# Values laid out block-diagonally, so that one matmul serves two heads

## The chip, the cores and the metric

The kernel runs on one core of a Trainium2 chip. The metric is the device time of one execution in microseconds. Before the change the median of three runs is 597.7 us (597.62 to 599.45). The engines are called TensorE (PE in the rows, its weight loads PEld), VectorE (DVE), ScalarE (ACT), GpSimd (POOL) and SyncE (SP); SyncE here only issues DMAs.

## The reference

Attention over chunks of 64 positions, then a mixture of eight experts that sends each row to its best expert:

```python
def _attn_ref(q, k, v):                      # (8 batches, 8 heads, 576, 64)
    ...                                      # 9 chunks of 64 positions each
    scores = scale * np.matmul(q_c, k_c.transpose(0, 1, 2, 4, 3))
    scores = scores - np.max(scores, axis=-1, keepdims=True)
    attn = np.exp(scores)
    attn = attn / (np.sum(attn, axis=-1, keepdims=True) + 1e-09)
    out = np.matmul(attn, v_c)

def _moe_ref(x, w_gate, w1, w2):             # x: 4608 rows of 512
    logits = x @ w_gate
    expert_idx = np.argmax(logits, axis=1)
    ...                                      # gate_w: softmax probability of that expert
    for e in range(E):
        h = np.maximum(x[expert_idx == e] @ w1[e], 0.0)
        out[expert_idx == e] = gate_w[expert_idx == e, None] * (h @ w2[e])
```

## The kernel before

The work has two parts. The **attention loop** takes 18 groups; a group (`G = 2` tiles of 128 rows) is 32 little attentions of 64 positions. Tile `i` of a group covers two chunks of positions (c = 0, 1, the two halves of the 128 output partitions) and eight heads, which are the pairs `hp` = 0 to 3 times the two halves m = 0, 1. The **slots** then run the experts: each gathers up to 384 rows of one expert and multiplies them with that expert's weights, which are split into a high and a low part (`w_hi`, `w_lo`), as the rows are (`xhi`, `xlo`), so that three fast products stand for one exact one.

In the attention loop everything is in fp32. A matmul in fp32 shows as two records, with two records of weight load. In iteration g, TensorE runs in this order: `scores(g)` (L237); selection of logits (L996); the transposes of the exponentials of group g - 1 (L282), which ScalarE copies to `at`; the transposes of the attention output of group g - 2 (L314); in some groups routing counts (L386 to L391); the value products `attn_v(g - 1)` (L291); and the logits of group g - 2 (L326). VectorE runs the maximum `mx` (L250), the subtraction that gives `ex` (L253), the sum `su` (L263), the reciprocal `ri` (L274), and `x_out`, which scales the products into the output tile (L303). ScalarE takes the exponential in place (L259).

Scores and value products use the 128x128 array as four tiles of 64x64: for each pair of heads four products (`quads`, L217), each 64 rows deep, 64 columns wide and with 64 moving columns. A group has 32 of these in `scores` and 32 in `attn_v`. The values lie as the keys do: m picks the lower or upper 64 partitions. `attn_v` writes m = 0 to PSUM bank U and m = 1 to bank V, so both banks are whole only at its end.

The order on TensorE, VectorE, ScalarE and GpSimd is the order of the program (`manual_schedule`). SyncE issues k and q of group g + 3 after `scores(g)`, and v of group g + 2 after `attn_v(g - 1)` (`load_qk`, `load_v`, L203 to L213, each DMA 256 KB); between them, a quarter of a weight chunk (`load_q`). Three buffers each for k, q and v.

TensorE's instructions are one long stream that is unrolled over the groups. Before the scores of group 3 the program aligns it (`addr_align`, L233).

In a slot, `gemm1` (L663) runs eight steps f; a step is 4 chunks `kc` times three products in the order high x high, high x low, low x high (`gemm1_pe`, L624). `xlo` is made by VectorE just before (`make_xt_x`, L609).

Of the kernel before, what the change touches and what calls it, by code (L numbers as in the profile page):

```python
# [18 lines left out]
P = 128  # L19
NT = 4608  # L20
D = 512
# [25 lines left out]
def attn_moe_kernel(ctx: ExitStack, tc: tile.TileContext, q, k, v, wg, w, out):  # L47
# [19 lines left out]
    raw = [wpool.tile([P, 2048], F32, name=f"raw{c}") for c in range(2)]  # L67
    w_hi = [None, None]
    w_lo = [None, None]
    w_hi[0] = [wpool.tile([P, 1024], F32R, name=f"whi0_{c}") for c in range(8)]  # L70
    w_lo[0] = [wpool.tile([P, 1024], F32R, name=f"wlo0_{c}") for c in range(8)]

    def split_chunk(par, c):
        hi, lo = w_hi[par][c], w_lo[par][c]
# [32 lines left out]
            t = t.rearrange("p (a b) -> p a b", b=shape[2])  # L107
        return t

    xtp = ctx.enter_context(tc.tile_pool(name="xtp", bufs=1))  # L110
    hp_ = ctx.enter_context(tc.tile_pool(name="hp", bufs=HB))
    xhi = xtp.tile([P, 4, BLK + EXT], F32R, name="xhi")
    xlo = xtp.tile([P, 4, BLK + EXT], F32R, name="xlo")
    gate = [const.tile([P, 3], F32, name=f"gate{i}") for i in range(3)]
    oid = [const.tile([P, 3], I32, name=f"oid{i}") for i in range(3)]

    NK, NB = 3, 3
    c1 = ExitStack()
    kv = c1.enter_context(tc.tile_pool(name="kv", bufs=1))
    qp = c1.enter_context(tc.tile_pool(name="qp", bufs=NK))  # L120
    sp = c1.enter_context(tc.tile_pool(name="sp", bufs=2))
    sm = c1.enter_context(tc.tile_pool(name="sm", bufs=2))


    xb = [kv.tile([P, RB, XW], F32, name=f"xb{i}") for i in range(XB - 1)] + [xg4]
    kb = [kv.tile([P, G, 512], F32, name=f"kb{i}") for i in range(NK)]
    vb = [kv.tile([P, G, 512], F32, name=f"vb{i}") for i in range(NB)]
    order = tc.manual_schedule(engines={
        mybir.EngineType.PE, mybir.EngineType.DVE, mybir.EngineType.Activation, mybir.EngineType.Pool})
    order.__enter__()  # L130
# [1 line left out]
    nc.vector.memset(ones, 1.0)  # L132

    pw = bank("U", [P, 4, P])
    warm = xhi[:, 0, EXT:WIDE]
    nc.vector.memset(warm.bitcast(F32), 1.0)
    for _ in range(WARM):
        nc.tensor.matmul(pw, ones, ones.unsqueeze(1).broadcast_to([P, 4, P]), start=True, stop=True)
    for n in (192, 192, 192, BLK, BLK, BLK):
# [4 lines left out]
    nc.gpsimd.iota(pid_i, pattern=[[P, NTILE]], base=0, channel_multiplier=1)  # L144
    wg_sb = kv.tile([P, 4, 32], F32, name="wg_sb")
    nc.gpsimd.memset(wg_sb, 0.0)
    for i in range(XB - 1):
        nc.gpsimd.memset(xb[i][:, :, D + 1:XW], 0.0)
    first = [sum(BATCHES[:i]) for i in range(NBAT + 1)]
    TE = [first[i] for i in EARLY]  # L150

# [49 lines left out]
    qt = {}  # L201

    def load_qk(g):  # L203
        t = qp.tile([P, G, 512], F32, name="qt")
        qt[g] = t

        for i in range(G):
            nc.sync.dma_start(kb[g % NK][:, i, :], k[g, :, i, :])
            nc.sync.dma_start(t[:, i, :], q[g, :, i, :])

    def load_v(g):
        for i in range(G):
            nc.sync.dma_start(vb[g % NB][:, i, :], v[g, :, i, :])  # L213

    def quads(i, hp):  # L217
        for c in range(2):
            for m in range(2):
                o = hp * 128 + c * 64  # L220
                yield (slice(c * 64, (c + 1) * 64), m, slice((i * 4 + hp) * 64, (i * 4 + hp + 1) * 64),
                       slice(m * 64, (m + 1) * 64), slice(o, o + 64), (m * 64, c * 64))
# [24 lines left out]
    def soft_a(ps):  # L247
        mx = sm.tile([P, NH, 1], F32, name="mx", bufs=2)
        ps3 = heads(ps)
        nc.vector.tensor_reduce(mx.rearrange("p h o -> p (h o)"), ps3, AX.X, ALU.max)  # L250

        ex = sp.tile([P, NH // 2, 2, 64], F32, name="ex", bufs=2)
        nc.vector.tensor_tensor(  # L253
            ex.rearrange("p h m k -> p m h k"), ps.rearrange("p m (h k) -> p m h k", k=64),
            mx.rearrange("p (m h) o -> p m h o", m=2).broadcast_to([P, 2, NH // 2, 64]), ALU.subtract)
        return ex

# [3 lines left out]
    def soft_c(ex):  # L261
        su = sm.tile([P, NH, 1], F32, name="su", bufs=2)
        nc.vector.tensor_reduce(su.rearrange("p (m h) o -> p m (h o)", m=2),  # L263
                                ex.rearrange("p h m k -> p m h k"), AX.X, ALU.add)
        return su

    def soft_e(su):
# [9 lines left out]
    def attn_t(ex, banks="UV"):  # L277
        at = sp.tile([P, G, 4, 128], F32, name="at", bufs=1)
        for i in range(G):
            pt = bank(banks, [P, 4, 128])  # L280
            for hp in range(4):
                nc.tensor.transpose(pt[:, hp, :], ex[:, i * 4 + hp, :, :].rearrange("p m k -> p (m k)"), ident)  # L282
            nc.scalar.copy(at[:, i, :, :], pt)
        return at

    def attn_v(g, at):
        px = [one["U"], one["V"]]
        for i in range(G):
            for hp in range(4):
                for po, m, fo, pi, fi, at_ in quads(i, hp):  # L290
                    nc.tensor.matmul(px[m][po, fo], at[pi, i, hp, po], vb[g % NB][pi, i, fi],  # L291
                                     start=True, stop=True, tile_position=at_)
        return px

    stored = set()
# [1 line left out]
    def x_out(g, px, ri, xt):  # L297
        r0 = g * G % RB

        t = g * G - XB * RB  # L300
        assert t < 0 or t in stored
        for m in range(2):
            nc.vector.tensor_tensor(  # L303
                xt[:, r0:r0 + G, m * 256:(m + 1) * 256].rearrange("p i (h d) -> p i h d", d=64),
                px[m].rearrange("p (i h d) -> p i h d", i=G, d=64),
                ri[:, m * NH // 2:(m + 1) * NH // 2, :].rearrange("p (i h) o -> p i h o", i=G)
                .broadcast_to([P, G, 4, 64]), ALU.mult)

    def x_t(g, xt):
        xT = sp.tile([P, 4, G * P], F32, name="xT1", bufs=1)  # L310
# [310 lines left out]
        nc.vector.tensor_tensor(xlo[:, :, 0:EXT], pg, o.bitcast(F32), ALU.subtract)  # L621
        ids(u, xg3, 2)

    def gemm1_pe(par, f, ph, part=range(4)):  # L624
        for kc in part:
            wh = w_hi[par][kc][:, f * 128:(f + 1) * 128]
            wl = w_lo[par][kc][:, f * 128:(f + 1) * 128]
            for i, (a, b) in enumerate(((wh, xhi), (wh, xlo), (wl, xhi))):
                nc.tensor.matmul(ph, a, b[:, kc, WIDE - ph.shape[1]:WIDE], start=kc + i == 0, stop=kc + i == 5)  # L629

    def low(o, ph, hi):
        nc.vector.scalar_tensor_tensor(o, ph, 0.0, hi.bitcast(F32), ALU.max, ALU.subtract)  # L632
# [30 lines left out]
    def gemm1(par, f, h, k, at_, more=None):  # L663
        ph = bank("X", [P, WIDE]) if f % 3 == 2 else bank("S", [P, WIDE])
        hi, lo, hx = h

        def wide(n):
            gemm1_pe(par, f, ph[:, WIDE - n:WIDE])
            if more is not None and n > BLK:
                more(n - BLK)  # L670

        by_kind(k, *(lambda n=n: wide(n) for n in (WIDE, BLK + EXT // 2, BLK)))
        nc.scalar.activation(hx[:, EXT:EXT + WIDE], ph, AF.Relu)  # L673
        low(lo, ph[:, EXT:WIDE], hi)
        low(hx[:, bass.ds(at_, EXT)], ph[:, 0:EXT], hx[:, EXT:2 * EXT])
# [95 lines left out]
    def scratch(shape):  # L771

        n = 1
        for x in shape[1:]:
            n *= x
        t = kb[0].rearrange("p g x -> p (g x)")[:, used[0]:used[0] + n]
        used[0] += n
        names = "abc"[0:len(shape) - 1]
        if len(names) > 1:
            t = t.rearrange(f"p ({' '.join(names)}) -> p {' '.join(names)}",  # L780
                            **{x: shape[i + 1] for i, x in enumerate(names) if i})
        return t
# [219 lines left out]
    def logits(g):  # L1002
        if g in st_x:
            lp, pp = logits_p(g, st_x.pop(g))
            nc.scalar.copy(lp, pp)
            st_l[g] = lp
# [26 lines left out]
    for g in range(NG):  # L1033
        ga, gl = g - 1, g - 2
        pace[0] = 1000
        if waiting:
            nc.gpsimd.tensor_copy(relay, st_l[gl - 1][:, 0:1])
        store(2 if g + 1 < NG else 4)
        ps = scores(g)
        keep((12, 6, 0)[min(g, 2)])  # L1040

        if gl >= 1:
            sel_(gl - 1)
            advance("c")
        if ga >= 0:
            at = attn_t(st_e[ga])
            su = soft_c(st_e.pop(ga))
        if gl >= 0:
            st_x[gl] = x_t(gl, xb[gl * G // RB % XB])
        if ga >= 0:  # L1050
            soft_e(su)
        st_e[g] = soft_a(ps)
        if g + 1 < NG:
            soft_b(st_e[g])
        else:

            c2.close()
            psum = ctx.enter_context(tc.tile_pool(name="psum", bufs=1, space=PSUM))
            slots["S"] = [psum.tile([P, 512], F32, name=f"psS{i}") for i in range(2)]
            turns["S"] = 0  # L1060
        pauses()
        for x in casts:
            next(x, None)
        casts.clear()
        advance("t")
        if g + 1 < NG:
            small_op(5)
        if ga >= 0:
            px = attn_v(ga, at)
        logits(gl)  # L1070
        cast(g)
        if g + 1 == NG:
            soft_b(st_e[g])
        if ga >= 0:
            ri = soft_d(su)
            x_out(ga, px, ri, xb[ga * G // RB % XB])
        small_op(2)
        advance("a")
        side_op(4)
        if g + 3 < NG:  # L1080
            load_qk(g + 3)
        if 3 <= g + 2 < NG:
            load_v(g + 2)
# [231 lines left out]
```

## Time and profile before

| | us |
|---|---|
| median of three runs | 597.7 (597.62 to 599.45) |
| the profiled execution's own time | 595.98 |
| its span, first to last instruction | 593.9 |
| TensorE busy in it | 559.2 (94%) |
| VectorE busy | 423.2 (71%) |
| ScalarE busy | 275.6 (46%) |
| GpSimd busy | 235.7 (40%) |

The first slices of the page show how the load shifts: DMA engines are nearly full over the first hundred microseconds, where q, k and v come in, and far from it later, while TensorE's digit is 7 to 9 throughout. "Busy" of TensorE counts an instruction from its start to its modelled end. The granted clock stands as a share of 2.4 GHz: 1.00 is 2.4 GHz, and 0.5 is 1.2 GHz; a mean between them says how much of the stretch was at either. A wait "for issue" is one for which the profile shows no cause.

### The profile page before, as it was taken

The page shows a single profiled execution, that of the slowest core. Times are in us where ns is not written, and L with a number is a line of the kernel's source. Part 1 is how long each engine was busy: PE and PEld are TensorE (multiplying, and loading weights), DVE is VectorE, ACT ScalarE, POOL GpSimd, SP SyncE. Part 2 cuts the span into 40 slices and gives each one's busy share as a digit, 9 for nine tenths or more (in the row PEclk, how much of TensorE's full clock was granted, in tenths as well). Part 3 has the DMA queues.
Part 4 walks back from the last instruction along what each step waited for, and adds up shares of the span by engine and source line. Part 5 has one row for each costly group of instructions (what it writes and reads, how often), then busy time and mean ns, then how long its engine had stood idle before and what let it go on. Part 6 is the DMA issues. An engine that isn't in the chain of part 4 may idle for free.

```text
span 593.9 us, 14394 instructions
## 1 busy us (share of the span) xinstructions
PE 559.2 (94%) x5323; PEld 492.7 (83%) x5323; DVE 423.2 (71%) x894; ACT 275.6 (46%) x475; POOL 235.7 (40%) x267
## 2 busy tenths in 40 slices
PE   8788888889899999999999999999999999999995
PEld 5676667678788898989999889989998989898984
DVE  6777787775586779689886787666756666765754
ACT  1466555555223456465654464353534344434432
POOL 3113433463733554535543344244422515242422
PEclk9899998787799999999999999999999999999998
DMA  8999997741455545223643452357542246220201
GB/s 288 366 324 300 357 370 254 265 147 47 174 191 197 205 133 176 61 76 120 218 157 119 146 199 81 124 167 253 167 178 72 86 149 221 67 66 21 72 1 55
DMA packets 53481, 99.10 MB, mean 167 GB/s; under 512 B 13696, under 2 KB 27008, under 8 KB 49792
## 3 DMA queue, kind: packets, MB, share of 16 engines
q0 software_dynamic: 18352, 58.30, 28.2%
q1 hardware_dynamic: 35024, 39.36, 20.4%
q8 instruction: 71, 1.16, 0.8%
q14 instruction: 34, 0.28, 0.1%
HBM read 106.59 MB, written 20.22 MB: 213 GB/s over the span
## 4 chain that ended last, share of the span: by engine, by line
PE 55%; issue 4%; SPq 2%; DMA 2%; POOL 2%; DVE 1%; POOLq 1%; ACT 0%; DVEq 0%
PE psS L629 21%; PE psL L629 7%; PE psV L722 4%; PE psU L724 4%; PE psV L723 3%; PE psV L724 3%; PE psU L723 3%; PE psU L722 3%; SPq L595 2%; PE psK L723 1%; PE psK L735 1%; PE psK L724 1%; PE psK L737 1%; PE psK L722 1%; DMA xg<-xd,idx 1%
## 5 line engine op out<-in xcount | busy, mean ns | idle before, releaser
L77 DVE TENSOR_TENSOR wlo<-raw,whi 128x1024 fp32r<-128x1024 f32 x110 | 134.0, 1218 | 16.5 <-ACT whi L76 11.5
L673 ACT ACTIVATE h<-psS 128x384 fp32r<-128x384 f32 x84 | 41.3, 492 | 168.1 <-issue 128.7
L538 POOL DMA_INDIRECT raw<-in_w,widx x58 | 68.7, 1184 | 125.8 <-DVE wlo L77 57.1
L629 PE MATMUL psS<-xlo,whi 128*128 128x256 f32 (+2 forms) x368 | 114.3, 311 | 1.1 <-DVE xlo L621 1.1
L629 PE MATMUL psS<-xhi,whi 128*128 128x256 f32 (+2 forms) x368 | 115.0, 312 | 0.1
L76 ACT CAST whi<-raw 128x1024 fp32r<-128x1024 f32 x110 | 114.8, 1044 | 0.1
L629 PE MATMUL psS<-xhi,wlo 128*128 128x256 f32 (+2 forms) x368 | 114.2, 310 | 0.0
L750 POOL DMA_INDIRECT out_y<-y,oid x40 | 42.3, 1058 | 106.8 <-ACTq L655 34.5
L632 DVE SCALAR_TENSOR_TENSOR hl<-psS,h 128x256 fp32r<-128x256 f32 x84 | 35.5, 422 | 62.4 <-ACT h L673 57.5
L629 PEld LDWEIGHTS psS<-xlo,whi 128*128 128x128 f32 x368 | 70.2, 191 | 4.6 <-DVE xlo L621 1.5
L629 PEld LDWEIGHTS psS<-xhi,whi 128*128 128x128 f32 x368 | 70.3, 191 | 4.2 <-ACT xhi L620 0.5
L556 POOL DMA_INDIRECT xg<-xd,idx x49 | 60.7, 1239 | 27.9 <-issue 15.7
L629 PEld LDWEIGHTS psS<-xhi,wlo 128*128 128x128 f32 x368 | 70.1, 191 | 0.0
L722 PE MATMUL psU<-whi,h 128*128 128x512 f32 x120 | 48.5, 404 | 0.0
L722 PE MATMUL psV<-whi,h 128*128 128x512 f32 x120 | 47.6, 397 | 0.0
L723 PE MATMUL psU<-wlo,h 128*128 128x512 f32 x120 | 47.3, 394 | 0.0
L723 PE MATMUL psV<-wlo,h 128*128 128x512 f32 x120 | 47.2, 393 | 0.0
L724 PE MATMUL psU<-whi,hl 128*128 128x512 f32 x112 | 44.2, 395 | 0.9 <-DVE hl L632 0.9
L724 PE MATMUL psV<-whi,hl 128*128 128x512 f32 x112 | 43.8, 391 | 0.0
L433 POOL DMA_INDIRECT xd<-xb,di x32 | 32.2, 1005 | 17.4 <-issue 10.1
L629 PE MATMUL psL<-xhi,wlo 128*128 128x320 f32 (+2 forms) x112 | 34.8, 311 | 0.0
L629 PE MATMUL psL<-xlo,whi 128*128 128x320 f32 (+2 forms) x112 | 34.8, 311 | 0.0
(251 smaller groups left out, 1151.8 us busy)
## 6 DMA issues: line engine op xcount, KB each, us to landing
kb<-in_k SPq DMA_DIRECT2D x36, 256.0 KB
qt<-in_q SPq DMA_DIRECT2D x36, 256.0 KB
vb<-in_v SPq DMA_DIRECT2D x36, 256.0 KB
xg<-xg SPq DMA_DIRECT2D x208, 32.0 KB
raw<-in_w SPq DMA_DIRECT2D x16, 256.0 KB
raw<-in_w,widx POOLq DMA_INDIRECT x58
xg<-xd,idx POOLq DMA_INDIRECT x49
out_y<-y,oid POOLq DMA_INDIRECT x40
```

What stands on the lines that cost most here:

```text
L76: nc.scalar.copy(hi, src)
L77: nc.vector.tensor_tensor(lo, src, hi.bitcast(F32), ALU.subtract)
L433: nc.gpsimd.indirect_dma_start(out=xds[t], out_offset=bass.IndirectOffsetOnAxis(ap=di[:, i, :], axis=0), in_=x, in_offset=None, bounds_che ...
L538: nc.gpsimd.indirect_dma_start(out=raw[c][:, :], out_offset=None, in_=w, in_offset=bass.IndirectOffsetOnAxis(ap=widx[:, u, c:c + 1], axis= ...
L556: nc.gpsimd.indirect_dma_start(out=t[:, :], out_offset=None, in_=xd[0:rows, :], in_offset=bass.IndirectOffsetOnAxis(ap=place(u, h), axis=0 ...
L629: nc.tensor.matmul(ph, a, b[:, kc, WIDE - ph.shape[1]:WIDE], start=kc + i == 0, stop=kc + i == 5)
L632: nc.vector.scalar_tensor_tensor(o, ph, 0.0, hi.bitcast(F32), ALU.max, ALU.subtract)
L673: nc.scalar.activation(hx[:, EXT:EXT + WIDE], ph, AF.Relu)
L722: nc.tensor.matmul(py, hh, wh, start=f == 0, stop=False)
L723: nc.tensor.matmul(py, hh, wl, start=False, stop=False)
L724: nc.tensor.matmul(py, hl, wh, start=False, stop=f == 7)
L750: nc.gpsimd.indirect_dma_start(out=outs[m], out_offset=bass.IndirectOffsetOnAxis(ap=oid[u % 3][:, m:m + 1], axis=0), in_=y, in_offset=None ...
```

## The change

1. The values lie block-diagonally. On the host, position s of half m goes to partition 2s + m. On the chip a buffer `vb` has two halves along the free axis; even partitions (m = 0) are filled in the first, odd ones (m = 1) in the second, and the rest is zero. One product of depth 128 then gives both heads of a pair: `attn_v` issues 16 products a group, 64 columns wide, with 128 moving columns, on two column tiles. It fills bank U with tile 0 and bank V with tile 1 of the group.
2. So that the transposed exponentials have the same order of partitions, `ex` holds the two halves interleaved (`h k m`); VectorE writes and reads it at a step of two elements.
3. The buffers of v are zeroed once at the start: the first by VectorE, the other two by GpSimd. `load_v` issues two DMAs as before, each of 64 partitions of 4 KB.
4. `x_out` goes by tile, not by half.
5. In a slot's first step the four products with `xlo` come after the other eight (`late=f == 0`).
6. `vb` has doubled, so memory is shared over time: k, q and one buffer of v lie in a pool `ep` that is closed in the last iteration, and `xhi`, `xlo`, the h tiles and the last weight chunk (`whi0_7`, `wlo0_7`) take its place. The scratch of the routing tables moves from `kb[0]` to `vb[0]`.

```diff
-    w_hi[0] = [wpool.tile([P, 1024], F32R, name=f"whi0_{c}") for c in range(8)]
+    w_hi[0] = [wpool.tile([P, 1024], F32R, name=f"whi0_{c}") for c in range(7)]
...
+    c3 = ExitStack()
+    ep = c3.enter_context(tc.tile_pool(name="ep", bufs=1, side="right"))
...
-    kb = [kv.tile([P, G, 512], F32, name=f"kb{i}") for i in range(NK)]
-    vb = [kv.tile([P, G, 512], F32, name=f"vb{i}") for i in range(NB)]
+    kb = [ep.tile([P, G, 512], F32, name=f"kb{i}") for i in range(NK)]
+    vb = [(ep if i == 1 else kv).tile([P, 2, G, 512], F32, name=f"vb{i}") for i in range(NB)]
...
     nc.vector.memset(warm.bitcast(F32), 1.0)
+    nc.vector.memset(vb[0], 0.0)
...
     nc.gpsimd.memset(wg_sb, 0.0)
+    nc.gpsimd.memset(vb[1], 0.0)
     for i in range(XB - 1):
         nc.gpsimd.memset(xb[i][:, :, D + 1:XW], 0.0)
+    nc.gpsimd.memset(vb[2], 0.0)
...
     def load_v(g):
-        for i in range(G):
-            nc.sync.dma_start(vb[g % NB][:, i, :], v[g, :, i, :])
+        for m in range(2):
+            nc.sync.dma_start(vb[g % NB][m::2, m, :, :], v[g, m::2, :, :])
...
-        ex = sp.tile([P, NH // 2, 2, 64], F32, name="ex", bufs=2)
+        ex = sp.tile([P, NH // 2, 64, 2], F32, name="ex", bufs=2)
         nc.vector.tensor_tensor(
-            ex.rearrange("p h m k -> p m h k"), ps.rearrange("p m (h k) -> p m h k", k=64),
+            ex.rearrange("p h k m -> p m h k"), ps.rearrange("p m (h k) -> p m h k", k=64),
...
             for hp in range(4):
-                for po, m, fo, pi, fi, at_ in quads(i, hp):
-                    nc.tensor.matmul(px[m][po, fo], at[pi, i, hp, po], vb[g % NB][pi, i, fi],
-                                     start=True, stop=True, tile_position=at_)
+                for c in range(2):
+                    po, o = slice(c * 64, (c + 1) * 64), hp * 128 + c * 64
+                    nc.tensor.matmul(px[i][po, hp * 128:(hp + 1) * 128], at[:, i, hp, po],
+                                     vb[g % NB][:, :, i, o:o + 64],
+                                     start=True, stop=True, tile_position=(0, c * 64))
...
-        for m in range(2):
+        r4 = ri.rearrange("p (m i h) o -> p i h m o", i=G, m=2)
+        for i in range(G):
             nc.vector.tensor_tensor(
-                xt[:, r0:r0 + G, m * 256:(m + 1) * 256].rearrange("p i (h d) -> p i h d", d=64),
-                px[m].rearrange("p (i h d) -> p i h d", i=G, d=64),
-                ri[:, m * NH // 2:(m + 1) * NH // 2, :].rearrange("p (i h) o -> p i h o", i=G)
-                .broadcast_to([P, G, 4, 64]), ALU.mult)
+                xt[:, r0 + i, 0:D].rearrange("p (m h d) -> p h m d", m=2, d=64),
+                px[i].rearrange("p (h m d) -> p h m d", m=2, d=64),
+                r4[:, i, :, :, :].broadcast_to([P, 4, 2, 64]), ALU.mult)
...
-    def gemm1_pe(par, f, ph, part=range(4)):
+    def gemm1_pe(par, f, ph, part=range(4), late=False):
...
-            for i, (a, b) in enumerate(((wh, xhi), (wh, xlo), (wl, xhi))):
-                nc.tensor.matmul(ph, a, b[:, kc, WIDE - ph.shape[1]:WIDE], start=kc + i == 0, stop=kc + i == 5)
+            parts = ((wh, xhi), (wh, xlo), (wl, xhi))
+            for i, (a, b) in enumerate(parts):
+                if not (late and i == 1):
+                    nc.tensor.matmul(ph, a, b[:, kc, WIDE - ph.shape[1]:WIDE], start=kc + i == 0,
+                                     stop=kc + i == 5 and not late)
+        if late:
+            for kc in part:
+                nc.tensor.matmul(ph, w_hi[par][kc][:, f * 128:(f + 1) * 128], xlo[:, kc, WIDE - ph.shape[1]:WIDE],
+                                 start=False, stop=kc == 3)
...
-            gemm1_pe(par, f, ph[:, WIDE - n:WIDE])
+            gemm1_pe(par, f, ph[:, WIDE - n:WIDE], late=f == 0)
...
+        if g + 1 == NG:
+            c3.close()
+            xtp = ctx.enter_context(tc.tile_pool(name="xtp", bufs=1, side="right", reuse_waits="tile"))
...
-    vh = chunks(v, "s")
+    vh = chunks(v, "s").reshape(NG, 2, 64, G, 512).transpose(0, 2, 1, 3, 4)
+    vh = np.ascontiguousarray(vh.reshape(NG, P, G, 512))
```

## Rows read from the trace of the kernel before

**Rows 1.** Stretches: from, to, length; busy (count) PE, PEld, DVE, ACT, POOL; clock; DMA.

```profile
17.10:127.30 110.20, 92.06 (x2382) 76.32 (x2378) 85.37 (x153) 60.17 (x132) 40.46 (x60) 0.91 0.87 306
...
200.00:565.00 365.00, 364.08 (x2033) 329.00 (x2032) 263.30 (x517) 174.86 (x259) 148.42 (x126) 1.00 0.41 132
```

**Rows 2.** The same view, from one group's scores to the next.

```profile
46.20:51.60 5.40, 5.40 (x169) 4.79 (x165) 5.23 (x12) 3.83 (x9) 1.27 (x1) 1.00 0.90 287
51.60:60.50 8.90, 6.66 (x160) 5.18 (x156) 6.25 (x10) 4.57 (x11) 4.03 (x7) 0.83 0.96 320
...
97.10:102.60 5.50, 5.45 (x163) 4.62 (x159) 5.25 (x11) 3.52 (x9) 2.16 (x3) 1.00 0.73 223
```

**Rows 3.** TensorE's waits, 17.1 to 127.3: who for whom: total, times, longest.

```profile
PE psS L237 <- issue: 5.2, 4, 1.9
...
PE psV L282 <- DVE mx L250: 2.2, 1, 2.2
...
PE psU L291 <- ACT at L283: 0.7, 1, 0.7
```

**Rows 4.** Stretches from the end of a wait to the next wait's start.

```profile
28.90:32.98 4.08, 4.08 (x126) 3.35 (x127) 2.03 (x4) 3.67 (x8) 0.00 (x0) 1.00 0.97 337
...
45.38:53.84 8.46, 8.46 (x254) 7.04 (x253) 7.79 (x16) 5.51 (x14) 2.46 (x6) 1.00 0.88 270
...
90.62:110.71 20.09, 19.96 (x508) 17.15 (x507) 16.96 (x38) 12.13 (x27) 7.03 (x13) 0.92 0.85 297
```

**Rows 5.** The page, DMA queues: packets, MB, share of the engines' span.

```profile
q8 instruction: 71, 1.16, 0.8%
```

**Rows 6.** TensorE's timeline in a group without a wait: start, length, instruction.

```profile
49.98 0.27 PE L291 MATMUL psU<-vb,at 64*64 64x64 f32 x1
...
50.73 0.22 PE L291 MATMUL psU<-vb,at 64*64 64x64 f32 x1
...
50.79 0.22 PE L291 MATMUL psU<-vb,at 64*64 64x64 f32 x1
...
51.07 0.64 PE L326 MATMUL psL<-xT,wg_sb 128*32 128x256 f32 x8
51.64 1.16 PE L237 MATMUL psS<-kb,qt 64*64 64x64 f32 x64
```

**Rows 7.** VectorE by line, 17.1 to 127.3: busy us, mean ns, idle before.

```profile
L253 DVE TENSOR_TENSOR ex<-psS,mx 128x1024 f32<-128x1024 f32 x15 | 18.4, 1225 | 0.5
...
L263 DVE TENSOR_REDUCE su<-ex 128x16 f32<-128x1024 f32 x15 | 18.1, 1209 | 0.0
L303 DVE TENSOR_TENSOR xb<-psU,ri 128x512 f32<-128x512 f32 x13 | 9.0, 692 | 9.0 <-PE psV L291 7.0 <-PE psU L291 1.4
...
L274 DVE RECIPROCAL ri<-su 128x16 f32<-128x16 f32 x14 | 3.5, 247 | 4.9 <-ACT su L269 4.9
```

**Rows 8.** VectorE's timeline at the start.

```profile
1.01 0.27 DVE L136 MEMSET xhi<- 128x256 f32 x1
1.20 1.48 DVE L160 CAST iota_f<-xg 128x128 f32<-128x128 int32 x1
...
5.30 0.16 DVE L192 TENSOR_SCALAR w_off<-iota_f 128x4 f32<-128x4 f32 x1
8.26 1.23 DVE L250 TENSOR_REDUCE mx<-psS 128x16 f32<-128x1024 f32 x1 [2.79 <-PE psS L237]
```

**Rows 9.** GpSimd's timeline at the start.

```profile
2.74 2.18 POOL L469 MEMSET xg<- 128x528 f32 x4
```

**Rows 10.** SyncE's DMA issues at the start.

```profile
2.61 0.91 SPq L213 DMA_DIRECT2D vb<-in_v  x2
```

**Rows 11.** TensorE's timeline at the first step of slot 1.

```profile
178.74 0.41 PE L629 MATMUL psS<-xlo,whi 128*128 128x320 f32 x1 [1.15 <-DVE xlo L621]
```

**Rows 12.** The chain that ended last, one step of gemm1: start, length, what.

```profile
290.28 1.43 PE psS L629 x12
```

More of the change, by code (lines that the diff above doesn't have):

```diff
@@ L69, in attn_moe_kernel @@
     w_lo = [None, None]
-    w_hi[0] = [wpool.tile([P, 1024], F32R, name=f"whi0_{c}") for c in range(8)]
-    w_lo[0] = [wpool.tile([P, 1024], F32R, name=f"wlo0_{c}") for c in range(8)]
+    w_hi[0] = [wpool.tile([P, 1024], F32R, name=f"whi0_{c}") for c in range(7)]
+    w_lo[0] = [wpool.tile([P, 1024], F32R, name=f"wlo0_{c}") for c in range(7)]
     def split_chunk(par, c):
@@ L108, in bank @@
         return t
[L110 to L113, printed above, removed]
     gate = [const.tile([P, 3], F32, name=f"gate{i}") for i in range(3)]
@@ L119, in attn_moe_kernel @@
     kv = c1.enter_context(tc.tile_pool(name="kv", bufs=1))
-    qp = c1.enter_context(tc.tile_pool(name="qp", bufs=NK))
+    c3 = ExitStack()
+    ep = c3.enter_context(tc.tile_pool(name="ep", bufs=1, side="right"))
     sp = c1.enter_context(tc.tile_pool(name="sp", bufs=2))
@@ L134, in attn_moe_kernel @@
     pw = bank("U", [P, 4, P])
-    warm = xhi[:, 0, EXT:WIDE]
+    warm = ep.tile([P, BLK], F32R, name="warm")
     nc.vector.memset(warm.bitcast(F32), 1.0)
+    nc.vector.memset(vb[0], 0.0)
     for _ in range(WARM):
@@ L203, in load_qk @@
     def load_qk(g):
-        t = qp.tile([P, G, 512], F32, name="qt")
+        t = ep.tile([P, G, 512], F32, name="qt", bufs=NK)
         qt[g] = t
@@ L263, in soft_c @@
         nc.vector.tensor_reduce(su.rearrange("p (m h) o -> p m (h o)", m=2),
-                                ex.rearrange("p h m k -> p m h k"), AX.X, ALU.add)
+                                ex.rearrange("p h k m -> p m h k"), AX.X, ALU.add)
         return su
@@ L281, in attn_t @@
             for hp in range(4):
-                nc.tensor.transpose(pt[:, hp, :], ex[:, i * 4 + hp, :, :].rearrange("p m k -> p (m k)"), ident)
+                nc.tensor.transpose(pt[:, hp, :], ex[:, i * 4 + hp, :, :].rearrange("p k m -> p (k m)"), ident)
             nc.scalar.copy(at[:, i, :, :], pt)
@@ L775, in scratch @@
             n *= x
-        t = kb[0].rearrange("p g x -> p (g x)")[:, used[0]:used[0] + n]
+        t = vb[0].rearrange("p m g x -> p (m g x)")[:, used[0]:used[0] + n]
         used[0] += n
@@ L1069, in attn_moe_kernel @@
             px = attn_v(ga, at)
+        if g + 1 == NG:
+            c3.close()
+            xtp = ctx.enter_context(tc.tile_pool(name="xtp", bufs=1, side="right", reuse_waits="tile"))
+            hp_ = ctx.enter_context(tc.tile_pool(name="hp", bufs=HB, side="right", reuse_waits="tile"))
+            xhi = xtp.tile([P, 4, BLK + EXT], F32R, name="xhi")
+            xlo = xtp.tile([P, 4, BLK + EXT], F32R, name="xlo")
+            for x, name in ((w_hi, "whi0_7"), (w_lo, "wlo0_7")):
+                x[0].append(xtp.tile([P, 1024], F32R, name=name))
         logits(gl)
```

## The prediction

> **What bounds the kernel now.** I went from the page's slices to the stretches (which part is limited by what), then to the groups of the loop, then to TensorE's waits, and last to single operations. From 200 us on nothing is to be won: TensorE is busy 364.08 of 365 us [rows 1]. The attention loop, from the scores of group 2 (17.1 us) to those of group 17 (127.3 us), is different: of its 110.2 us TensorE is idle 18.1 (110.20 less 92.06), and the granted clock is 0.91 on average, which is 9.9 us more work than at 2.4 GHz [rows 1]. A group at full clock without a wait takes 5.4 to 5.5 us; the one from 51.6 takes 8.9, with a clock of 0.83 [rows 2]. So the loop holds 15 x 5.5 = 82.5 us of work and 27.7 us of waiting and half clock. It is TensorE's loop, not the DMA's: the largest wait in it that is neither for "issue" nor for mx is 0.7 us, for ScalarE [rows 3].
>
> Those waits have one odd feature: most are put down to "issue", nothing that the profile shows [rows 3]. They sit in the middle of runs of equal instructions. The page's wait for VectorE's mx, 2.2 us, is of the same kind: it splits the transposes of one tile, which wait for nothing new. Counting instructions gives the cause: between the end of one such wait and the start of the next lie 253 or 254 of TensorE's matmuls and weight loads, or twice or four times as many [rows 4] (ten such stretches follow each other; the first, a double one and the last are shown). With two or three semaphore waits that is 256. The instruction queue brings 1.16 MB in 71 packets [rows 5], 16.3 KB each. So TensorE waits for its own code, block by block. From 28.9 to 90.62 us eleven blocks take 61.7 us, 5.6 each (the first and the last row give the ends), while a group, (2382 + 2378)/15 = 317 instructions, does its work at 5.5 x 253.5/317 = 4.4 us a block. The code arrives slower than it is used.
>
> The Trainium skill, Runtime: NRT & Kernel Launch, section Instruction fetch mechanics, says that code comes in 16 KiB blocks of 256 instructions, fetched while the last is run, and calls the crossing "mostly hidden". The block size agrees with the counts above; that it is hidden does not, in this loop. By the page fewer instructions would buy nothing; that is the second rival below.
>
> **The change, part by part.**
>
> *Value products.* 32 products of 64x64 become 16 of 128x64 with 128 moving columns; half of what they multiply is zero. Each product is two records of matmul and two of weight load, so a group drops 64 of its 317 instructions: 253, and with its waits about one block of code. A block now has a group's whole work to arrive in.
>
> The products themselves get longer. Now they last from 49.98 to 51.07, 1.09 us: four records go at once, a step of four takes 0.058 (50.73 to 50.79), 16 steps are 0.93, and 0.16 goes on entry and exit [rows 6]. The new ones are not in the trace. The logits use column tiles side by side: eight records of 256 columns in four column tiles take 0.57 us from first start to the next line (51.07 to 51.64); less 0.16 that is two steps of 0.2, so about 0.105 to 0.115 for 128 columns [rows 6]. With two column tiles, 32 records are 16 steps of 0.11: 1.76 + 0.16 = 1.9 us, 0.8 more than now. From below: if the step is set by issuing (0.058 for four, so 0.029 for two) it is 0.46 + 0.16, 0.5 less than now. From above: no overlap, 32 x 0.11 + 0.16 is 3.7 us, 2.6 more. I take 0.8, since the logits are the nearest operation.
>
> A clean group then takes 6.3 us, more than the 5.6 that a block took. The loop's work is 15 x 6.3 = 94.5. I leave 0.2 us a group for fetches that are late (3.0) and one stretch at half clock (1.5, as 0.17 x 8.9 in [rows 2]): 99.0. **Saved in the loop: 11.2 us.** If the code came in no faster than 6.9 us a block, 6.7.
>
> *Around the loop.* The products of groups 0, 16 and 17 lie outside these 15 intervals: 3 x 0.8 = 2.4, of which I expect some 0.4 back from waits: **+2.0**.
>
> *ex with the two heads interleaved.* VectorE writes and reads it at a step of 8 bytes, same counts. Its six operations take 5.3 us a group (1.23 for ex, 1.23 for mx, 1.21 for su, 0.69 for each half of x_out, 0.25 for ri) [rows 7, 8], below 6.3 even with the routing's small ones. The rows show 1.2 ns an element, from PSUM and from SBUF alike, so I take 0; at worst both SBUF sides double, +2.4 us a group on VectorE; a gain has no reason, since no element is dropped. x_out's halves become ready one after the other, the first at half of the products: it ends when it did, within 0.1.
>
> *v's loads.* Two DMAs as before, 64 partitions of 4 KB for 128 of 2 KB, same bytes, same place in SyncE's queue. I take 0. At worst they slow down the other loads, and that is the first rival; a gain of 1 or 2 us through faster code fetches is as possible.
>
> *Zeroing vb.* VectorE zeroes 2048 columns before its constants: 256 columns took 0.27 us, so 2.2 [rows 8]. GpSimd zeroes 4096, at 2.18/4 for 528: 4.3 us [rows 9], and is next needed far later. SyncE issues v of group 0 at 2.61 [rows 10] and would wait to about 3.5, with k and q of group 1 behind it; 1 MB before them is still on its way, so the DMA engines do not run dry. VectorE's constants ended at 5.46 and its first softmax began at 8.26 [rows 8]: 2.8 us of cover for 2.2. But a cast of 128 columns took 1.48 us beside GpSimd's work, so the constants may be held up. **+0.5**, between 0 and 2.5.
>
> *Low parts last in a slot's first step.* Slot 1 waited 1.15 us for xlo [rows 11]. Eight other products now come first, at 1.43/12 each [rows 12]: **-0.95**. No later slot has such a wait.
>
> *Memory.* xhi, xlo, h and the last weight chunks now lie where kb, qt and vb lay. They wait for the scores of 17 and the products of 16, which stand earlier on TensorE than what fills them: 0. If that cover were gone, one ACT copy would stall for about a microsecond.
>
> **Sum.** -11.2 + 2.0 + 0.5 - 0.95 = -9.65 us. The profiled execution took 595.98 (span 593.9 and 2.1 around it), so 586.3; the median of the runs is 597.7, 1.7 above it: **588.0 us**. What comes after the loop is TensorE's own queue or hangs on the routing of the last batch, so it moves along.
>
> **The rivals.**
> - *The code still comes late.* The loads of a group now come every 6.3 us, not 7.35, at a DMA share that is already 0.87 over the loop [rows 1]; the code queues with them. For it: in most single groups the share is 0.9 and more [rows 2]. Against it: the last third of the loop has no weight loads. At 6.9 us a block: 597.7 - 6.7 + 1.55 = 592.5, and up to 597 with the half-clock stretches kept.
> - *The waits do not go by the number of instructions* (slower). If they come by time, as from data or semaphores, the 27.7 us stay and each product run costs 0.8 more: 15 x 0.8 + 2.0 + 0.5 - 0.95 = +13.6, 611. Against it: the counts of [rows 4]. The Trainium skill's page Runtime: NRT & Kernel Launch, section Instruction fetch mechanics, would lead to this one. It decides if the products' place stalls as often as now.
> - *The two column tiles do not run together* (slower). 2.6 a group: 15 x 8.1 = 121.5 without a wait, +11.3, and 7.8 outside the loop: about 616. It decides from 1.85 us a group on (27.7/15). Against it: the logits' overlap.
> - *VectorE at a step of 8 bytes* (slower). From about 0.5 us on each of the two operations VectorE sets the pace; at the worst bound 7.7 a group: 115.5, +5.3, and with the rest 605.
> - *The blocks' edges move in the slots.* 18 x 64 instructions fewer shift all later edges. Sixteen blocks lie in 200 to 565 us with no wait now [rows 1]; if each showed 0.3 us, +5: 593.
>
> **How the numbers follow.** Forecast 0.62, its own range 583 to 593; late code 0.18; by time 0.05; no overlap 0.04; VectorE 0.05; edges 0.06. About 0.3% (1.8 us) is what a measurement of this kernel tells from no change. Faster: 0.62, nine tenths of the late code, most of the edges: 0.83. Same 0.05, slower 0.12. The range goes from 582 (no fetch late, no half clock: 4.5 below the forecast and a little for the loads) to 597, which leaves the slow cases out.
>
> **What would show it.** Right: the loop shows 15 blocks, not 19, few "issue" waits above 0.5 us, a clock near 1.0, groups of 6.2 to 6.5 us; products of 1.8 to 2.0 us; mx, ex and su within 2% of now; the wait at slot 1 gone. Wrong: waits still 256 instructions apart and over a microsecond; products above 2.5 us; ex above 1.5 us; idle TensorE after 200 us.

## The result, and the profile after

The changed kernel takes **579.15 us** (579.00 to 580.26, 4 runs) where the kernel before takes 598.39 (597.62 to 599.45, 4 runs): ratio 0.968, 95% interval 0.966 to 0.970. It is faster, as forecast, but by 19.2 us in place of 9.65, and below the range's low end of 582. The profiled run took 580.26 (span 578.2, against 593.9). These two profiles are 15.7 us apart, since the one before lies 2.4 us below its kernel's median and the one after 1.1 above. In them the time went like this:

| stretch | before | after | difference | forecast |
|---|---|---|---|---|
| start, to the scores of group 2 | 17.1 | 19.8 | +2.7 | +1.3 (0.5 for zeroing, 0.8 for group 0's products) |
| loop, to the scores of group 17 | 110.2 | 89.6 | -20.6 | -11.2 |
| the rest | 466.6 | 468.8 | +2.2 | +0.25 (1.6 for two groups' products, 0.4 back, 0.95 for slot 1) |

On three other chips the kernel before took other times: its median was 586.5 (583.4 to 595.3), 586.9 (579.2 to 598.4) and 595.0 us (589.9 to 597.7), the changed one's 573.5, 573.6 and 576.8 beside it; the ratios are 0.978 (0.974 to 0.982), 0.983 (0.976 to 0.989) and 0.970 (0.966 to 0.975). The ratios leave out slow runs, those over 1.5% above a kernel's fastest on that chip; the medians and ranges hold all. So 1.7 to 3.2% is gained, depending on the chip, and the kernel before spreads up to 19 us where the changed one spreads 3.

The stretches of the changed kernel: the loop, a plain group, one with routing, and slots. They answer to [rows 1, 2].

```profile
19.80:109.40 89.60, 89.57 (x1898) 77.40 (x1896) 84.17 (x148) 59.49 (x132) 33.78 (x50) 1.00 0.98 354
49.10:55.00 5.90, 5.90 (x128) 5.08 (x124) 5.45 (x8) 4.15 (x10) 3.62 (x4) 1.00 0.85 282
79.00:85.20 6.20, 6.20 (x137) 5.46 (x133) 5.87 (x14) 3.74 (x8) 2.60 (x6) 1.00 0.96 342
182.00:549.00 367.00, 366.33 (x2037) 330.20 (x2036) 263.88 (x518) 175.93 (x261) 143.50 (x125) 1.00 0.41 131
```

Read the first line against its counterpart: TensorE's idle time went from 18.1 us to 0.03, its clock from 0.91 to 1.00, its matmul records from 2382 to 1898. All that [rows 3] lists is gone: the view of TensorE's waits is empty for the loop. In the slots nothing new appears. The page's line on the queue that brings code, where [rows 5] had 71 packets:

```profile
q8 instruction: 67, 1.10, 0.8%
```

A group's value products, to the logits that follow (the answer to [rows 6]), and VectorE's write of `ex` (to [rows 7]):

```profile
76.51 1.09 PE L292 MATMUL psU<-vb,at 128*64 128x128 f32 x16
77.43 1.04 PE L292 MATMUL psV<-vb,at 128*64 128x128 f32 x16
78.41 0.64 PE L328 MATMUL psL<-xT,wg_sb 128*32 128x256 f32 x8
```

```profile
L253 DVE TENSOR_TENSOR ex<-psS,mx 128x1024 f32<-128x1024 f32 x15 | 18.5, 1234 | 0.5
```

From 76.51 to 78.41 is 1.90 us, the forecast to the digit; `ex` at a step of 8 bytes costs 0.7% more.

VectorE's start (to [rows 8]), the same `ident` before the change, GpSimd beside it after the change, and TensorE's second scores:

```profile
1.66 1.76 DVE L134 MEMSET vb<- 128x2048 f32 x1 [0.38 <-issue]
3.34 1.89 DVE L160 CAST iota_f<-xg 128x128 f32<-128x128 int32 x1
5.29 3.26 DVE L164 TENSOR_SCALAR ident<-iota_f,pid 128x128 f32<-128x128 f32 x1
10.06 1.22 DVE L250 TENSOR_REDUCE mx<-psS 128x16 f32<-128x1024 f32 x1
```

```profile
2.74 0.62 DVE L164 TENSOR_SCALAR ident<-iota_f,pid 128x128 f32<-128x128 f32 x1
```

```profile
3.35 1.79 POOL L148 MEMSET vb<- 128x2048 f32 x1
6.04 1.96 POOL L471 MEMSET xg<- 128x528 f32 x4
```

```profile
12.60 1.63 PE L237 MATMUL psS<-kb,qt 64*64 64x64 f32 x64 [2.83 <-DVE ex L253]
```

The zeroing itself takes 1.76 us, but `ident`, 0.62 us before the change, now takes 3.26, to 8.55: GpSimd, set back by its share of `vb`, is zeroing until 8.47. The first softmax starts at 10.06 in place of 8.26, and TensorE waits for it.

### The profile page after: what moved, and what is told of

It reads as the page before. It is cut to its first block, busy times and chain, and to the rows that moved or that the text cites. A ratio compares the mean times of both kernels' runs of the same rounds, so it can differ in the third digit from the quotient of the medians.

```text
span 578.2 us, 13238 instructions
## 1 busy us (share of the span) xinstructions
PE 558.7 (97%) x4747; PEld 493.1 (85%) x4747; DVE 432.8 (75%) x895; ACT 275.6 (48%) x475; POOL 233.4 (40%) x269
## 4 chain that ended last, share of the span: by engine, by line
PE 72%; issue 4%; DVE 1%; POOL 1%; ACT 1%; another core or an unknown queue 0%; POOLq 0%; DVEq 0%; ACTq 0%
PE psS L633 25%; PE psL L633 8%; PE psU L733 5%; PE psU L731 5%; PE psV L731 5%; PE psV L733 4%; PE psU L732 4%; PE psV L732 4%; PE psK L744 2%; PE psK L746 2%; PE psS L637 1%; PE psK L731 1%; PE psK L733 1%; PE psK L732 1%; PE psT L616 1%
## 5 line engine op out<-in xcount | busy, mean ns | idle before, releaser
L540 POOL DMA_INDIRECT raw<-in_w,widx x58 | 64.5, 1111 | 130.1 <-DVE wlo L77 57.1
L633 PE MATMUL psS<-xhi,wlo 128*128 128x256 f32 (+2 forms) x368 | 113.0, 309 | 0.0
L633 PE MATMUL psS<-xlo,whi 128*128 128x256 f32 (+2 forms) x312 | 96.6, 309 | 0.3 <-DVE xlo L584 0.3
L759 POOL DMA_INDIRECT out_y<-y,oid x40 | 41.0, 1026 | 110.3 <-ACTq L664 34.7
L558 POOL DMA_INDIRECT xg<-xd,idx x49 | 60.8, 1240 | 29.1 <-issue 15.7
L633 PEld LDWEIGHTS psS<-xlo,whi 128*128 128x128 f32 x312 | 58.9, 189 | 3.4 <-DVE xlo L584 0.5
L633 PE MATMUL psL<-xhi,whi 128*128 128x320 f32 (+2 forms) x112 | 34.9, 312 | 0.0
```

What stands on the lines that cost most here:

```text
L540: nc.gpsimd.indirect_dma_start(out=raw[c][:, :], out_offset=None, in_=w, in_offset=bass.IndirectOffsetOnAxis(ap=widx[:, u, c:c + 1], axis= ...
L558: nc.gpsimd.indirect_dma_start(out=t[:, :], out_offset=None, in_=xd[0:rows, :], in_offset=bass.IndirectOffsetOnAxis(ap=place(u, h), axis=0 ...
L759: nc.gpsimd.indirect_dma_start(out=outs[m], out_offset=bass.IndirectOffsetOnAxis(ap=oid[u % 3][:, m:m + 1], axis=0), in_=y, in_offset=None ...
```

## The experiments

The theory: TensorE's code comes in blocks of 256 instructions; before the change a block is used up faster than the next one comes, and after it no longer. Rivals: the waits do not go by the length of the code, or they are the data's. Each loop below is read from the profile of one execution.

**More code, no more work.** Dead code that is jumped over, in the changed kernel, in every group after group 3 (63 slots, in pad128 twice as many):

```diff
     def scores(g):
-        if g == 3:
+        if 3 <= g < NG:
             nc.tensor.addr_align(64, offset=48, max_nops=0)
+            if g > 3:
+                nc.tensor.addr_align(64, offset=47, max_nops=0)
+                nc.tensor.addr_align(64, offset=46, max_nops=0)   # pad128 alone
```

> The changed kernel with 63 dead code slots and an alignment in every group from the fourth on: a group takes 320 slots of TensorE's code (384 where a batch is routed) in place of 256, jumped over, with no matmul more. Theory (TensorE's code arrives in blocks of 256, behind the data, and is used faster than it comes): about 1.3 blocks a group at 4.6 to 5.6 us a block give groups of 6.1 to 7.4 us, waits put down to nothing ('issue') come back, the loop of 89.6 us grows to between 93 and 111, the whole by 3 to 20 us. Rival (the gain came from the products' new shape or from the data, the length of code is immaterial): within 1 us of the changed kernel, no new waits.

> As the last one, with 126 dead slots: 384 slots a group (448 with routing), about 1.6 blocks. Theory: groups of 7.3 to 8.9 us, the loop between 109 and 133, the whole slower than the kernel before (by up to 25 us). Rival: as the changed kernel within 1 us.

589.96 us (587.4 to 593.7) and 608.5 (605.0 to 610.4) beside 583.4 for the kernel before; the changed kernel itself was not run on this chip. Their loops, and their largest waits (first pad64, then pad128):

```profile
19.80:128.70 108.90, 94.39 (x1896) 80.85 (x1894) 87.59 (x150) 60.39 (x132) 34.97 (x51) 0.97 0.87 295
```

```profile
PE psU L284 <- issue: 9.3, 4, 2.8
PE psS L239 <- issue: 4.6, 3, 2.1
```

```profile
19.80:144.80 125.00, 102.17 (x1894) 87.87 (x1892) 87.94 (x155) 60.92 (x132) 36.60 (x56) 0.90 0.76 258
```

```profile
PE psS L240 <- issue: 13.2, 5, 3.0
PE psV L285 <- issue: 2.9, 1, 2.9
```

With the same matmuls the loop grows from 89.6 (90.6 at most on the chips where the changed kernel ran) to 108.9 and 125.0; the waits without a cause are back, and the clock falls again. One group of 256 slots, ten of 320 and four of 384 are 19.5 blocks: 5.6 us each. With 384 and 448 they are 23: 5.4 us each. Before it was 5.6. The time per block is nearly constant, the time per group is not. The queue of the two brings 71 and 75 packets in place of 67. Counted with the dead slots, all waits of over 1.1 us in the two loops stand at one and the same place of a block, wherever in a group that falls: in pad64 80 or 144 instructions after a jump, in pad128 17, 81 or 145. (Three of 0.4 to 1.1 us stand at a jump, where the edge of a block lies in the dead slots.) So it is the blocks, not the jumps: the theory holds, and the rival that the length of the code does not matter is out.

The branch alone, with up to 7 dead slots (`addr_align(8, ...)` in every group):

> The changed kernel with an alignment to 8 slots in every group: the branch over dead code that the two padded kernels have, with at most 7 dead slots. Theory: loop within 0.5 us of 89.6, so it was the length of the code, not the branch, that cost 19 and 35 us there. Rival (branches stop the fetching): several us longer.

574.4 us (one run), loop 91.7; the changed kernel beside it has 90.6 (one late block of 0.41 us in it). That is more than the 0.5 us over 89.6 that was expected, but far from 19 and 35: by these two profiles the branch costs about a microsecond in the loop.

**Half the products.** In the kernel before:

```diff
-                for po, m, fo, pi, fi, at_ in quads(i, hp):
+                for po, m, fo, pi, fi, at_ in list(quads(i, hp))[0:2]:
                     nc.tensor.matmul(px[m]
```

> The kernel before with only the first 64 rows of each value product computed: 16 products of 64x64 a group in place of 32 (half of the attention's output is left out). A group has 253 instructions and 0.55 us less work, 4.6 us. Theory: the same number of blocks as the changed kernel, so nearly all of the 27.7 us of waits and half clock go although the block's work is shorter; the groups are then held by code or data at 4.9 to 5.6 us, the loop at 74 to 84. Rival (waits do not go by the number of instructions): 110.2 less 15 x 0.55, 102.

564.6 us; the loop:

```profile
16.00:104.60 88.60, 81.94 (x1905) 68.53 (x1901) 84.55 (x149) 58.90 (x133) 33.34 (x50) 1.00 1.01 371
```

The waits for code go with the instructions (1.5 us of them is left). The rest of the expectation failed. Half of the products saved no time of their own: 32 records on two of the array's four tiles took 1.08 us a group, as the 64 on all four did (1.09). And a group with 0.82 us less in its products than the changed kernel's (1.90) is only 0.07 us shorter (88.6 against 89.6 in all), over the 74 to 84 expected: something else sets about 5.9 us. Data (371 GB/s, share 1.01) or VectorE: the next runs tell.

**Less data.** In the kernel before, first v alone, then k and q too:

```diff
-            load_qk(g + 3)
+            qt[g + 3] = qt[g]        # no_data alone
-        if 3 <= g + 2 < NG:
+        if 3 <= g + 2 < 5:           # no_data: never
             load_v(g + 2)
```

> The kernel before without loading v from group 5 on (old values are used again): a quarter fewer bytes for k, q and v in the loop, the same 317 instructions a group. Theory (code queues behind data): blocks come faster than the 5.6 us of before, the loop of 110.2 shrinks to between 83 and 95. Rival (a block takes its time whatever the data do): 110 within 3.

> The kernel before with k, q and v loaded for groups 0 to 2 alone and used again (the later groups compute old values), so that in the loop hardly more than the weights is moved. Theory (the packets of code queue behind data): the time from the entry of a block to the packet of the next falls from a mean of 2.8 to 3.0 us to below 1, a block needs some 3 us, the waits of 256 instructions go and the loop falls to 81 to 86 us. Rival (fetching has a latency of its own, which data lengthen little; a quarter less data only brought 2.5): the time to the packet stays at 2 to 2.5, a block takes 4.6 to 5, the waits stay with shorter lengths, the loop is 87 to 95 us.

Without v the loop is 100.5 us, between what the two expected; the totals (595.8 and 550.8, one run each) say nothing, since old values route the rows differently. The loop without v, then the loop with hardly any data, TensorE's largest wait in it, and all that VectorE waited for from 28 us on:

```profile
16.10:116.60 100.50, 85.71 (x2395) 72.17 (x2386) 83.85 (x149) 60.20 (x133) 35.67 (x55) 0.95 0.79 265
```

```profile
16.40:106.90 90.50, 81.57 (x2384) 67.75 (x2379) 84.41 (x149) 59.22 (x131) 35.79 (x55) 1.00 0.30 106
```

```profile
PE psS L237 <- DVE ex L253: 3.4, 8, 0.8
```

```profile
DVE ri L274 <- ACT su L269: 1.5, 2, 1.1
```

Here each 256th instruction of TensorE was set against the starts of the packets on the instruction queue. (It brings other engines' code too, so which packet is TensorE's is read from the order.) From entering a block to the packet of the next took 2.8 us in the mean before (3.0 on another chip), 2.5 without v, about 1 without data. From a packet's start to the first use of its code, where TensorE waited for it, 2.2 to 2.8 us passed in nearly every case (two of 3.0 and 3.3), in these kernels and the padded ones. So a fetch needs about 5.1 us beside the loop's data and 3.2 without them (estimates, 2.8 and 1 plus some 2.2 to 2.3), and the work of a block of the kernel before lasts 4.1 to 4.4. In the changed kernel the packet came 2.3 us after the block was entered, and its code was used 2.8 us after that at the earliest. From 28 us on no wait for code is left. The loop nevertheless stays at 90.5, 6.0 a group: TensorE now waits for VectorE's `ex`, and VectorE is busy 84.41 of 90.50 (5.6 a group: the 5.3 of the prediction and the small operations of routing) and from 28 us on it waits 1.5 us for ScalarE and, by the view, not for TensorE. So neither code nor data: **VectorE holds a group at about 6 us**. The first expectation (81 to 86) had missed that; the rival's 87 to 95 holds the number, but its reason, a slow fetch and waits that stay, was not there.

**The other parts.** The changed kernel again on other chips, the kernel before with a profile, and `late=False`:

> The changed kernel once more, beside the kernel before on this chip: the study before this one was on a chip where the kernel before took 583.4 us (its undisturbed runs from 580.3) in place of 598. If the gain is that of code that no longer comes late, it is the smaller the less late the code came: the changed kernel is at 577 to 581 on either chip, and the gain lies between 0.5 and 3.3%. Rival (a fixed part, as fewer instructions to carry out): 3.2% on every chip.

> The kernel before, for its profile on the chip of this call. Theory: where it is faster than 598, its loop is shorter (95 to 105 us for 110.2) with fewer or shorter waits 256 instructions apart, and the rest of it unchanged at 466 within 3. Rival (it is faster elsewhere): the loop stays at 110.

> The changed kernel with the low parts back in their old order in a slot's first step. Theory: slot 1 waits about 1.15 us for xlo again, 0.7 to 1.2 us slower than the changed kernel. Rival: the wait had been an accident of the profiled execution, no difference (within 0.3).

573.46 us, 583.41 (before, 8 runs) and 573.88. The loops of the kernel before and of the changed kernel on this chip:

```profile
16.50:122.10 105.60, 84.89 (x2394) 71.59 (x2385) 85.13 (x149) 59.72 (x133) 35.68 (x55) 0.97 0.90 316
```

```profile
19.40:109.00 89.60, 89.58 (x1894) 77.41 (x1892) 84.18 (x148) 59.52 (x132) 33.41 (x50) 1.00 0.98 356
```

The loop of the changed kernel is the same on both chips, that of the kernel before 4.6 us shorter on the second, where it has less half clock (0.97 for 0.91). But the rest is shorter there too: 459.3 for 466.6, and 462.2 for 468.8 in the changed kernel. So the first expectation, that the difference between chips lies in the loop (95 to 105) and the rest stays at 466 within 3, was only half right.

Without the late low parts (no_late) slot 1 waits as before:

```profile
154.77 0.41 PE L633 MATMUL psS<-xlo,whi 128*128 128x320 f32 x1 [1.16 <-DVE xlo L623]
```

The rest is 1.4 us longer in the profile than in the changed kernel's, the medians differ by 0.4, within the runs' spread of 2.5: the wait is shown, its worth in the whole is not resolved.

**The start.** Three orders of the zeroing and of the first loads, in the changed kernel. First, all of it on GpSimd, behind its other work, and k and q of groups 0 and 1 loaded ahead of v of group 0:

```diff
-    nc.vector.memset(vb[0], 0.0)
-    nc.gpsimd.memset(vb[1], 0.0)
-    nc.gpsimd.memset(vb[2], 0.0)
...
-    for g in range(3):
-        load_qk(g)
-        load_v(g)
+    load_qk(0)
+    load_qk(1)
...
     nc.gpsimd.memset(xg3, 0.0)
+    for i in range(3):
+        nc.gpsimd.memset(vb[i], 0.0)
+    load_v(0)
+    load_qk(2)
+    load_v(1)
+    load_v(2)
```

> The changed kernel with all three value tiles zeroed by GpSimd after its other work of the start, and k and q of groups 0 and 1 loaded ahead of v of group 0. Theory (VectorE's constants are held by the zeroing, and with them the first softmax): mx of group 0 starts at 7.2 to 8.3 us in place of 10.06, TensorE's wait of 2.83 us goes, scores of group 2 start at 16.5 to 17.3 in place of 19.8, the whole is 2.5 to 3.2 us shorter. Rival (the loop is held by its data, DMA share 0.98): the loop grows by what the start gains, no difference in the whole.

575.55 us (573.3 to 578.7) beside 573.5 for the changed kernel: 2.1 longer in the median, not 2.5 to 3.2 shorter. mx starts at 8.44, but SyncE issued v of group 0 only at 11.35, behind k and q of later groups, and TensorE pays for it (SyncE's row, then TensorE's):

```profile
11.35 4.16 SPq L210 DMA_DIRECT2D vb<-in_v  x6
```

```profile
17.54 1.97 PE L289 MATMUL psU<-vb,at 128*64 128x128 f32 x16 [3.10 <-DMA vb<-in_v]
```

Then, GpSimd zeroes the first buffer right after its iotas, the others before its work on `xg`:

```diff
-    nc.vector.memset(vb[0], 0.0)
+    nc.gpsimd.memset(vb[0], 0.0)
     wg_sb = kv.tile([P, 4, 32], F32, name="wg_sb")
...
+    for i in (1, 2):
+        nc.gpsimd.memset(vb[i], 0.0)
```

> The changed kernel with vb of group 0 zeroed by GpSimd first of all and the other two after its small constants, nothing of it on VectorE; the loads in the order of the changed kernel. Theory (the zeroing holds VectorE's constants, and in the study before v of group 0 came too late behind k and q): v of group 0 is issued at about 3 us as before, the constants end by 8.3, mx of group 0 starts at 8.2 to 8.6 in place of 10.06, scores of group 2 at 16.3 to 17.5, the whole is 2 to 3 us shorter than the changed kernel. Rival: GpSimd's zeroing holds VectorE as long wherever it stands, mx still near 10, no difference.

> The changed kernel once more, for the comparison with the last one on the same chip: its loop 89.6 us as on the two chips so far, the whole between 572 and 581.

574.2 beside 573.6: no difference. mx starts at 10.60, for a reason that this row of VectorE shows, with GpSimd's last zeroing of `vb` under it.

```profile
1.20 6.72 DVE L158 CAST iota_f<-xg 128x128 f32<-128x128 int32 x1
```

```profile
4.29 3.54 POOL L467 MEMSET vb<- 128x2048 f32 x2
```

The cast that took 1.48 us [rows 8] was held for 6.72, to 7.92, while GpSimd zeroed without a pause to 7.83: the rival was right. Last, ScalarE zeroes the first buffer, GpSimd the others at its end, and SyncE's first loads keep the program's order:

```diff
-    nc.vector.memset(vb[0], 0.0)
+    nc.scalar.activation(vb[0].rearrange("p m g x -> p (m g x)"),
+                         ones[:, 0:1].broadcast_to([P, 4 * 512]), AF.Copy, scale=0.0)
...
+    with tc.manual_schedule(engines={mybir.EngineType.SP}):
+        load_qk(0); load_qk(1); load_v(0); load_qk(2); load_v(1); load_v(2)
```

> The changed kernel with vb of group 0 zeroed by ScalarE, which has nothing to do until 12.6 us, the other two by GpSimd after all its work of the start; SyncE's first loads kept in the order k and q of groups 0 and 1, v of 0, k and q of 2, v of 1 and 2. Theory (VectorE is held whenever GpSimd's work goes on without a pause: a cast took 6.72 us there): constants end at 5.5, mx of group 0 starts at 8.2 to 8.6, v of group 0 is there before the products, scores of group 2 start at 16.3 to 17.5, the whole is 1.5 to 3 us shorter than the changed kernel beside it. Rival (what the start gains is given back in the loop, whose blocks of code and data then come later): the loop longer than 91.5, no difference.

> The changed kernel again, for the comparison with the last one on the same chip: 572 to 581.

**575.0 us** (574.4 to 575.6) beside 576.8 (575.0 to 578.0) for the changed kernel; against the kernel before 0.967 (0.963 to 0.971) and 0.970 (0.966 to 0.975). ScalarE's zeroing takes 1.91 us, unseen; mx starts on time, and so do the scores of group 2 (rows of ScalarE, VectorE, TensorE):

```profile
2.04 1.91 ACT L134 ACTIVATE vb<-ones 128x2048 f32<-128x2048 bf16 x1
```

```profile
7.85 1.22 DVE L248 TENSOR_REDUCE mx<-psS 128x16 f32<-128x1024 f32 x1 [0.67 <-PE psS L235]
```

```profile
15.99 1.16 PE L235 MATMUL psS<-kb,qt 64*64 64x64 f32 x64
```

They start at 16.0 in place of 17.6 (19.8 on the first chip), the loop stays at 89.7. The start's 1.6 us is shown; its worth in the whole is not resolved: the intervals of the two ratios overlap, and in the two profiles the rest is 1.1 us longer.

## Why the prediction was wrong in size

*The mechanism.* Right. Waits of 256 instructions, a code that comes slower than it is used, 64 instructions fewer a group, about one block a group: each was seen, and dead code brought the waits back. The Trainium skill, Runtime: NRT & Kernel Launch, section Instruction fetch mechanics, calls the crossing of a block "mostly hidden". The changed kernel agrees (no wait in 89.6 us), the kernel before does not (some 16 of its 18.1 us idle stand at edges of blocks); what decides here is whether a block's work outlasts the fetch, some 5.1 us.

*The step that failed: "A clean group takes 6.3 us".* It took 5.90. The loop came out 9.4 us below the 99.0 that were forecast; 4.9 of them are this step's (94.5 for the work, measured 89.6), 4.5 the next one's. The products came out as said (1.90); the base of 5.5 to which their 0.8 was added was too long. The groups it was read from were not clean. The one from 46.2 holds 0.42 us of routing, from this row to the products at 49.98 [rows 6]:

```profile
49.56 0.19 PE L386 MATMUL psK<-oh_b,tri 128*128 128x56 bf16 x1
```

Without it, it is 5.0; those from 97.1 and 102.6 hold 0.4 of pauses in their products (1.49 us in place of 1.09). TensorE's own work was 5.0 to 5.1, plus 0.8 is 5.9. Fifteen times 0.4 is 6 us, less about 1 for the four groups with routing (6.2). The runs say more: without waits for code the old products would not have given groups of 5.1 either, but 6.0, VectorE's pace (no_data; half gives 5.9). So, as far as no_data stands for a loop with data, the longer products cost nothing; they fill what TensorE would have waited for VectorE. The prediction had compared VectorE's 5.3 with 6.3 and left it there; with routing and its waits VectorE needs 6.

*The second mis-sized term: 4.5 us for late fetches and half clock.* It was 0 here (0.41 us in one of the four profiles of the changed kernel). A block now lasts 6.0 us against some 5.1 for a fetch, which could have been worked out from the packets' times in the trace before; the prediction took the block's mean of 5.6, which already contained the waiting.

*The start.* Forecast +0.5 for the zeroing, measured 1.8 at mx and 2.7 in all with group 0's products. The cover of 2.8 us in [rows 8] was right for VectorE's own 1.76 (2.2 forecast), and GpSimd's 4096 columns (4.2 by [rows 9], not 4.3) took 3.58; the constants that GpSimd holds were named, but not priced. On its chip start_4 is 1.6 us ahead of the changed kernel at the scores of group 2.

*Low parts last.* The wait of 1.15 [rows 11] went, and came back with the old order. *ex, v's loads, memory, block edges in the slots:* 0, as forecast: TensorE is busy 366.33 of 367 us there.

*The rest* grew by 2.2 (2.9 on the second chip) for 0.25. Two groups' products explain 1.6, slot 1 gives 1.15 back; about as much is a wait of 1.1 to 1.6 us of group 17's transposes for VectorE's `xb`, which was not forecast. Against it stands the clock in the 32.7 us behind the loop, 0.79 in the kernel before and 0.91 in the changed one on the first chip. In the changed kernel's first profile there is also this wait:

```profile
136.84 1.02 PE L1005 MATMUL psL<-sel_g,lp 128*128 128x8 f32 x4 [3.47 <-ACT lp L1014]
```

ScalarE itself had waited 2.54 us, put down to "remote"; on two other chips the same wait is 0.49, on the last one 2.3 us are lost just ahead of it. What that is stays open, as does why the rest differs by 7 us between chips for either kernel.

Of the rivals, none came true; the late code (592.5) would have needed blocks of 6.9 us.

## What to carry to other kernels

Where TensorE stalls without a cause, count its instructions between the stalls; if it is a constant, compare the work in one block of code with the time from entering it to the next block's use. Fewer, longer instructions are then free up to the next bound, and that bound (here VectorE) is to be worked out before the cost of the longer ones is added. A "clean" group has to be taken apart by lines before it becomes the base of a sum.

## What was not expected of the hardware

- From the start of a packet of code to its first use 2.2 us passed at least wherever TensorE waited for it; the time before the packet fell from 2.8 to about 1 us when the loop's data went.
- A VectorE cast was held for 6.72 us beside GpSimd's consecutive zeroing, where it took 1.48 beside a shorter run of GpSimd's small operations; VectorE's own zeroing (1.76 beside GpSimd's), and mx and ex (1.23 and 1.25 beside it, in start) were not held. The Trainium skill, SBUF — State Buffer, section SBUF: two separate sides, describes a port pair that GpSimd and certain VectorE operations lock against each other, for a whole instruction. The row agrees with a lock, but the hold lasted over several GpSimd instructions; that this port pair is the cause, no run here isolates.
- 32 records of 128 columns on two column tiles take 1.90 us, where transposes of 128 columns on the whole array follow each other every 0.109 us in the trace before (32 of them, 3.5): they do run side by side.
